# Attention into a soft mixture of experts: other bank shares for the value products, and sums moved off VectorE

## The chip, the cores and the metric

One core of a Trainium2 chip runs the program. Its engines work side by side, each through its own list of instructions in the order written: TensorE (PE in the rows; PEld is its weight load), VectorE (DVE), ScalarE (ACT), GpSimd (POOL); SyncE (SP) starts most transfers. Matrix products land in PSUM, which is cut into banks of 512 fp32 columns a partition; POOL works on SBUF only here. The metric is the device time of one execution in microseconds (us), lower is better.

## The reference

```python
def _attn_ref(q, kv, w_sr):
    kv_pool = kv.reshape(B, H // r, r, W // r, r, C).mean(axis=(2, 4))
    kv_flat = kv_pool.reshape(B, -1, C) @ w_sr      # 768 keys, used as values too
    s = (q @ k.transpose(0, 2, 1)) / sqrt(C)
    a = exp(s - s.max(-1)); a /= a.sum(-1) + 1e-09
    return a @ v

def _moe_ref(x, phi, w1, w2):
    logits = x @ phi                                 # 32 slots
    d = exp(logits - logits.max(0)); d /= d.sum(0) + 1e-09   # over all tokens
    slot_input = d.T @ x
    slot_out = relu(slot_input[e] @ w1[e]) @ w2[e]   # 8 experts, 4 slots each
    c = exp(logits - logits.max(1)); c /= c.sum(1) + 1e-09   # over the slots
    return c @ slot_out
```

There are 4 batches of 12288 queries with 128 channels (49152 tokens in all). The slot part needs the attention output of all tokens before any output can be written.

## The kernel before

Queries go in 96 blocks of 512 (index `i`), four blocks to a group of 16 tiles of 128 tokens (index `g`; 23 groups of four blocks, one of three, one of one: 25 in all, 0 to 24). For each block:

- `qk` (L553 to L562): scores, transposed, six key tiles of 128 keys by 512 queries, each from three fp32 products, into three PSUM tiles `s_0` to `s_2` of two banks each.
- `rowmax1` to `rowmax4` on DVE with one small product `rowmax_pe` (L598) between: the maximum of each query over all keys. `rowmax2` puts a small array into the last 80 columns of one of two shared banks `m0` and `m1`, `rowmax_pe` writes its 64 columns there (the key `pq` in the plan), `rowmax3` (L603) reads them back.
- `sub` (L616, DVE), `exp_hi` and `exp_t` (ACT), `plo` (L633, POOL): the exponentials as a sum of two fp16 arrays.
- `av_hi` and `av_lo` (L645 to L658): for each of the block's four tiles of 128 queries, 12 products with the high parts and 6 with the low part of the exponentials, 161 columns wide (row sum, 128 channels, 32 slot logits). They collect in `m0` or `m1`, two tiles (322 columns) to a bank (key `px`), and ACT copies each pair to `xl` with `av_evac` (L668).

For each group, `g0` to `g7a` keep running slot sums: the logits `LL`, their maximum over the group (`g2`, `g2c`, a small product `g3m` in a shared bank, key `pc`, then `g3` and `g3r` on DVE), rescaled exponentials (POOL, ACT), 32 products `g7m` (L834) in a shared bank (key `pd`) and the addition `g7a` to `acc` (DVE). For the output softmax, `k_max` (DVE), `k_sub` (POOL), `k_exp` (ACT), `k_sum` (L869, DVE), `k_add` (L874, ACT), `k_rec` (L879, DVE) and `k_mul` (L884, POOL) turn a group's logits into weights.

When all groups are through, the tail computes the slots' experts (`t_psi` to `t_slo`) and then 25 output chunks, one per group: transposes `c_t`, high and low parts `c_hi` (L1418, ACT) and `c_lo` (DVE), products `o_mm`, two copies `o_ev` (one half of each chunk by ACT, L1448, one by DVE, L1450), and a transfer of 1 MB (`o_dma`, L1468).

The order on PE, DVE, ACT and POOL is fixed when the program is built. The class `Plan` takes each piece of work with an estimated cost, a priority and its dependences, plays the engines against each other and writes the pieces down in the order in which they got their turn. `m0` and `m1` are handed out there too: `bank` chooses the one that is free first by the plan. A piece with `fill` waits for a gap until it is due. On the chip each engine then keeps that order whatever the pieces really take. `JOIN` says how many groups share one `k_add` and one `k_rec`.

Of the kernel before, what the change touches and what calls it, by code (L numbers as in the profile page):

```python
# [33 lines left out]
SPARE = 0.02  # L34


class Plan:
# [22 lines left out]
    def emit(self):  # L60
# [31 lines left out]
        def bank(key):  # L92
            found = []
            for b in range(len(banks)):
                if key[0] == "pq":
                    t = gone(banks[b])
                    beside = banks[b] is not None and banks[b][1][0] == "px" and t == inf
                    if beside:
                        t = summed.get(banks[b], inf)
                    found.append((max(t, gone(tops[b])), not beside, b))  # L100
                else:
                    found.append((max(gone(banks[b]), gone(tops[b])), False, b))
            return min(found)

        def acquire(n, now):
# [10 lines left out]
            if ops[n][0] == "ACT":  # L116
                for key in ops[n][11]:
                    if key[0] == "m" and key[1][0] == "px":
# [89 lines left out]
def attention_then_soft_moe(ctx: ExitStack, tc: tile.TileContext, qT, kv0, kvT, w_sr, w_srT, phi, w1, w2, outT):  # L208
# [111 lines left out]
    MRUN = {}  # L320
    NBK = BQ // Q32
# [16 lines left out]
    KEEP = 5  # L338
    SPAN = 2
    KPS = 2  # L340
    KSD = 2
# [3 lines left out]
    JOIN = (0, AHEAD, 12, EARLY)  # L345
# [10 lines left out]
    LATE = 6.0  # L356
# [278 lines left out]

    def av_tile(i, k):
        if k % 2 == 0 and i == NB - 1:
            PX[i, k // 2] = ps.tile([P, 2, BQ], F32, tag=f"s{k // 2}", name=f"px_{i}_{k}")[:, :, :VW]
        elif k % 2 == 0:
            px = mt([P, 512], f"px_{i}_{k}")  # L640
            PX[i, k // 2] = px[:, : 2 * VW].rearrange("p (n c) -> p n c", n=2)
        return PX[i, k // 2][:, k % 2, :]

    def av_hi(i, k, t0):
        _, vhi, vlo = VU[i // BPB]  # L645
        px = PX[i, k // 2][:, k % 2, :] if t0 else av_tile(i, k)
        ks = slice(k * P, (k + 1) * P)
        for t in range(t0, t0 + AVS):
            p = PP[i, t // TH][0][:, t % TH, ks]
            nc.tensor.matmul(px, p, vhi[:, t, :], start=(t == 0 and (i >= AHD or k % 2 == 0)), stop=False)  # L650
            nc.tensor.matmul(px[:, 1:], p, vlo[:, t, :], start=False, stop=False)  # L651

    def av_lo(i, k):
        vhi = VU[i // BPB][1]
        px = PX[i, k // 2][:, k % 2, :]
        ks = slice(k * P, (k + 1) * P)
        for t in range(NT):
            nc.tensor.matmul(px, PP[i, t // TH][1][:, t % TH, ks], vhi[:, t, :], start=False, stop=(t == NT - 1 and (i >= AHD or k % 2 == 1)))  # L658

    def av_evac(i, k):  # L660
# [3 lines left out]
        o = (i - GB[g][0]) * TB + 2 * k  # L664
        if i == NB - 2 and k == 0:
            nc.vector.tensor_copy(XL[g][:, o : o + 2, :], PX.pop((i, k)))
        else:
            nc.scalar.activation(XL[g][:, o : o + 2, :], PX[i, k], AF.Copy)  # L668
# [113 lines left out]
    def g3(g):  # L782
        d = G[g]
        c1 = sm2(g, "c1", [P, 1])
        nc.vector.tensor_reduce(out=c1, in_=d["pc"][:, :NQD], axis=X, op=ALU.max)
        d["gm"] = d["pc"][:, NS : 2 * NS]
        nc.vector.transpose(out=d["gm"], in_=c1.broadcast_to([P, NS]))

    def g3r(g):
        d = G[g]  # L790
        MRUN[g] = gp.tile([P, NS], F32, tag="mrun", name=f"mrun_{g}", bufs=3)
        if g == 0:
            nc.vector.tensor_copy(MRUN[g], d["gm"])
        else:
            nc.vector.tensor_tensor(out=MRUN[g], in0=MRUN[g - 1], in1=d["gm"], op=ALU.max)

# [41 lines left out]

    def g7a(g):
# [5 lines left out]
        nc.vector.tensor_tensor(out=acc, in0=acc, in1=G[g]["pd"][:, : C + 1], op=ALU.add)  # L845


    def k_max(g, u=None):
        o, n = GB[g][0] * TB, nt(g)
        if u is not None:  # L850
            o, n = o + u * TB, TB
# [12 lines left out]
    def k_sum(g, u=None):  # L864
# [4 lines left out]
        nc.vector.tensor_reduce(out=RM[:, o : o + n], in_=LL[:, o : o + n, :], axis=X, op=ALU.add)  # L869

# [167 lines left out]
    def group_ops(g):  # L1038
# [28 lines left out]
        def go(name, eng, cost, dep, f, acq=(), use=(), path=None, fill=False):  # L1067
            k[0] += 1
            due = base + step * k[0] + LATE if fill and not fast else None
# [26 lines left out]
        go("3c", "DVE", 0.42, [o["3m"]], g3, use=[mc], fill=True)  # L1096
        go("3", "DVE", 0.19, [o["3c"]] + ([ops["g3", g - 1]] if g else []), g3r, use=[mc], fill=True)
# [13 lines left out]
        go("7a", "DVE", 0.25, [o["7m"]] + prev, g7a, use=[md], fill=True)  # L1111
# [7 lines left out]
    def av_rest(i, k, m, p, prev):  # L1119
        los = [ops["lo", i, 0], ops["lo", i, 1]]  # L1120
        a2 = end_lo = op("PE", 6 * 0.072, 0.17, p + 0.8, prev + los, lambda: av_lo(i, k), use=[("plo", (i, 0)), ("plo", (i, 1)), m])
        if k % 2:
            g = GOF[i]
            first = i == GB[g][0] and k == 1
            x = ("xl", g)
            if i == NB - 1:
                v = k // 2
# [4 lines left out]
            ops["x", i, k // 2] = op(  # L1132
# [481 lines left out]
```

## Time and profile before

| what | value |
|---|---|
| median of 3 runs | 1062.12 us (1062.01 to 1062.18) |
| profiled execution, its own time | 1062.19 us |
| its span, first to last instruction | 1060.4 us |
| PE busy | 1027.6 us (97%) |
| DVE busy | 971.5 us (92%) |
| POOL busy | 872.5 us (82%) |
| ACT busy | 793.6 us (75%) |
| granted TensorE clock | 0.996 of full speed, the level of 2.4 GHz |

The span has three parts: a start of some 25 us, the 96 blocks until about 976 us, and the tail. The page's shares are means over all three. PE's busy time counts a product from its start to its end, and neighbours overlap, so a lost moment is read from the distance between two starts.

### The profile page before, as it was taken

The page shows a single profiled execution, that of the slowest core. Times are in us where ns is not written, and L with a number is a line of the kernel's source. Part 1 is how long each engine was busy: PE and PEld are TensorE (multiplying, and loading weights), DVE is VectorE, ACT ScalarE, POOL GpSimd, SP SyncE. Part 2 cuts the span into 40 slices and gives each one's busy share as a digit, 9 for nine tenths or more (in the row PEclk, how much of TensorE's full clock was granted, in tenths as well). Part 3 has the DMA queues.
Part 4 walks back from the last instruction along what each step waited for, and adds up shares of the span by engine and source line. Part 5 has one row for each costly group of instructions (what it writes and reads, how often), then busy time and mean ns, then how long its engine had stood idle before and what let it go on. Part 6 is the DMA issues. An engine that isn't in the chain of part 4 may idle for free.

```text
span 1060.4 us, 24836 instructions
## 1 busy us (share of the span) xinstructions
PE 1027.6 (97%) x10261; PEld 880.3 (83%) x10261; DVE 971.5 (92%) x1552; ACT 793.6 (75%) x1046; POOL 872.5 (82%) x509
## 2 busy tenths in 40 slices
PE   8999999999999999999999999999999999999994
PEld 5788888888888888888888888888888888888452
DVE  6989999999999999999999999999999999998774
ACT  3777887888777787788787787788787787776463
POOL 0789998889989988889989988889988999895800
PEclk9999999999999999999999999999999999999998
DMA  9234510120137320120146310120110110112598
GB/s 370 112 83 89 119 54 3 42 87 15 41 72 148 71 56 2 41 100 2 41 87 134 86 41 1 41 100 1 41 41 2 42 41 1 41 41 91 198 416 368
DMA packets 15729, 89.17 MB, mean 84 GB/s; under 512 B 1664, under 2 KB 1920, under 8 KB 9344
## 3 DMA queue, kind: packets, MB, share of 16 engines
q1 hardware_dynamic: 11728, 69.47, 17.8%
q0 software_dynamic: 3312, 17.70, 8.9%
q8 instruction: 81, 1.33, 0.5%
q10 hardware_dynamic: 576, 0.41, 0.1%
q14 instruction: 32, 0.26, 0.1%
HBM read 58.87 MB, written 25.17 MB: 79 GB/s over the span
## 4 chain that ended last, share of the span: by engine, by line
PE 86%; DVE 7%; DMA 3%; ACT 1%; issue 1%; POOL 0%; SPq 0%; DVEq 0%; ACTq 0%; POOLq 0%
PE m L650 15%; PE m L658 14%; PE m L651 14%; PE s L560 12%; PE s L562 12%; PE s L561 11%; DMA outT<-o 2%; PE m L834 2%; DVE r L578 2%; DVE t L616 2%; PE po L1434 1%; DMA kv<-kv 1%; PE m L1406 1%; DVE m L603 1%; PE m L465 1%
## 5 line engine op out<-in xcount | busy, mean ns | idle before, releaser
L633 POOL TENSOR_TENSOR plo<-t,phi 128x1536 f16<-128x1536 f32 x190 | 599.0, 3163 | 92.9 <-ACT t L628 84.0
L624 ACT ACTIVATE phi<-t 128x1536 f16<-128x1536 f32 x192 | 283.5, 1478 | 148.0 <-DVE t L616 148.0
L578 DVE TRANSPOSE_TENSOR_REDUCE r<-s 128x32 f32<-128x1024 f32 x289 | 354.0, 1234 | 8.4 <-PE s L562 1.6
L650 PE MATMUL m<-vhi,phi 128*128 128x161 f16 x2280 | 353.2, 234 | 8.2 <-DVE m L603 7.3
L651 PE MATMUL m<-vlo,phi 128*128 128x160 f16 x2280 | 352.4, 233 | 0.0
L616 DVE TENSOR_TENSOR t<-s,mb 128x1024 f32<-128x1024 f32 (+1 forms) x384 | 342.0, 950 | 6.2
L628 ACT ACTIVATE t<-t 128x1536 f32<-128x1536 f32 x192 | 283.1, 1476 | 1.2
L650 PEld LDWEIGHTS <-phi 128*128 128x128 f16 x2304 | 224.1, 98 | 21.7 <-issue 21.3
L560 PE MATMUL s<-qhi,khi 128*128 128x512 f32 x574 | 237.0, 413 | 0.6 <-DVE t L616 0.4
L651 PEld LDWEIGHTS <-phi 128*128 128x128 f16 x2304 | 225.1, 98 | 12.1 <-issue 10.6
L562 PE MATMUL s<-qhi,klo 128*128 128x512 f32 x574 | 224.6, 391 | 0.0
L561 PE MATMUL s<-qlo,khi 128*128 128x512 f32 x574 | 223.9, 390 | 0.0
L658 PE MATMUL m<-vhi,plo 128*128 128x161 f16 x2280 | 223.5, 234 | 0.0
L658 PEld LDWEIGHTS <-plo 128*128 128x128 f16 x2304 | 171.9, 98 | 2.8 <-issue 2.7
L550 POOL TENSOR_TENSOR qlo<-q,qhi 128x512 fp32r<-128x512 f32 x95 | 127.5, 1342 | 23.9 <-ACT qhi L545 23.9
L562 PEld LDWEIGHTS s<-qhi,klo 128*128 128x128 f32 x574 | 107.7, 188 | 23.7
L560 PEld LDWEIGHTS s<-qhi,khi 128*128 128x128 f32 x574 | 107.9, 188 | 21.7 <-issue 2.6
L561 PEld LDWEIGHTS s<-qlo,khi 128*128 128x128 f32 x574 | 108.2, 189 | 19.4 <-issue 0.7
L668 ACT ACTIVATE xl<-m 128x322 f32<-128x322 f32 x189 | 81.3, 430 | 50.4 <-PE m L658 44.1
L608 DVE STREAM_TRANSPOSE mb<-m 128x512 f32<-128x512 f32 x96 | 68.3, 712 | 3.3
L545 ACT ACTIVATE qhi<-q 128x512 fp32r<-128x512 f32 x96 | 59.5, 620 | 2.8 <-DMA q<-qT 2.7
L603 DVE TENSOR_REDUCE m<-m 128x16 f32<-128x64 f32 x96 | 21.5, 224 | 22.6 <-PE m L598 19.2
(196 smaller groups left out, 840.4 us busy)
## 6 DMA issues: line engine op xcount, KB each, us to landing
q<-qT SPq DMA_DIRECT2D x23, 1024.0 KB, 4.9
outT<-o SPq DMA_DIRECT2D x22, 1024.0 KB, 8.3
kva<-kvT POOLq DMA_DIRECT2D x9, 1536.0 KB, 11.6
kva<-kvT SPq DMA_DIRECT2D x3, 1536.0 KB, 12.8
kv<-kv SPq DMA_DIRECT2D x6, 512.0 KB, 6.2
w<-w SPq DMA_DIRECT2D x2, 1536.0 KB, 6.3
w<-w SPq DMA_DIRECT2D x4, 768.0 KB, 4.1
kva<-kva POOLq DMA_DIRECT2D x3, 768.0 KB, 10.8
```

The source lines that it names most:

```text
L550: eng.tensor_tensor(out=lo, in0=q_src(i), in1=hi.bitcast(F32), op=ALU.subtract)
L560: nc.tensor.matmul(s, khi[:, ks], hi, start=True, stop=False)
L561: nc.tensor.matmul(s, khi[:, ks], lo, start=False, stop=False)
L562: nc.tensor.matmul(s, klo[:, ks], hi, start=False, stop=True)
L578: nc.vector.tensor_reduce(out=MX[i][:, t : t + n, :].rearrange("p t b -> p (t b)"), in_=S[i, t // 2][:, u : u + n, :].rearrange("p t (b j) ...
L616: nc.vector.tensor_tensor(out=TT_[i, h][:, o : o + n, :], in0=S[i, t // 2][:, u : u + n, :], in1=MX[i].unsqueeze(1).broadcast_to([P, n, BQ ...
L624: nc.scalar.activation(hi, TT_[i, h], AF.Exp, scale=SCALE)
L628: nc.scalar.activation(t, t, AF.Exp, scale=SCALE)
L633: eng.tensor_tensor(out=lo, in0=TT_.pop((i, h)), in1=PP[i, h][0], op=ALU.subtract)
L650: nc.tensor.matmul(px, p, vhi[:, t, :], start=(t == 0 and (i >= AHD or k % 2 == 0)), stop=False)
L651: nc.tensor.matmul(px[:, 1:], p, vlo[:, t, :], start=False, stop=False)
L658: nc.tensor.matmul(px, PP[i, t // TH][1][:, t % TH, ks], vhi[:, t, :], start=False, stop=(t == NT - 1 and (i >= AHD or k % 2 == 1)))
```

## The change

1. The four tiles of a block share the banks as three and one (483 and 161 columns) instead of two and two (`part`, `px_of`, `av_evac`). The plan lets the row maxima's columns (`pq`) stand beside a single value tile, a `pc` or a `pd`, no longer beside a pair (`BESIDE`).
2. `k_sum` of groups 4 to 21 leaves DVE. A chain of five POOL additions per group, `k_tree`, takes its place; it may start once `g5m` of group 23 is done, that is, in the tail. `JOIN` goes from three shared steps to seven.
3. `g7a` of groups before 23 becomes a copy on ACT (`g7e`) and an addition on POOL.
4. The running slot maximum is kept as one column (`CM`): `g3r` takes a maximum of two columns and then the transpose into `MRUN`.
5. `k_max` of a group is two DVE instructions instead of four.
6. `g3m` of groups 1 to 20 waits for the third score tile five blocks on, and `g7m` for the last one six blocks on.

```diff
+BESIDE = ("pc", "pd")
...
-                    beside = banks[b] is not None and banks[b][1][0] == "px" and t == inf
+                    beside = banks[b] is not None and (banks[b][1][0] in BESIDE or banks[b][1][0] == "px" and banks[b][1][2] == 1) and t == inf
...
-    JOIN = (0, AHEAD, 12, EARLY)
+    JOIN = (0, AHEAD, 6, 9, 12, 15, 18, EARLY)
...
+    def part(i, k):
+        if i == NB - 1:
+            return k // 2, k % 2, 2
+        return (0, k, TB - 1) if k < TB - 1 else (1, 0, 1)
...
-            nc.scalar.activation(XL[g][:, o : o + 2, :], PX[i, k], AF.Copy)
+            nc.scalar.activation(XL[g][:, o : o + n, :], PX[i, k], AF.Copy)
...
     def g3r(g):
-        d = G[g]
+        if g:
+            nc.vector.tensor_scalar_max(CM[g], CM[g], CM.pop(g - 1))
         MRUN[g] = gp.tile([P, NS], F32, tag="mrun", name=f"mrun_{g}", bufs=3)
...
+        nc.vector.transpose(out=MRUN[g], in_=CM[g].broadcast_to([P, NS]))
...
+    def g7e(g):
+        d = G[g]
+        d["px"] = sm2(g, "pdx", [P, C + 1])
+        nc.scalar.activation(d["px"], d["pd"][:, : C + 1], AF.Copy)
...
-        nc.vector.tensor_tensor(out=acc, in0=acc, in1=G[g]["pd"][:, : C + 1], op=ALU.add)
+        nc.gpsimd.tensor_tensor(out=acc, in0=acc, in1=G[g]["px"], op=ALU.add)
...
+    def k_tree(g):
+        o, n = GB[g][0] * TB, nt(g)
+        t = gp.tile([P, TG, NS], F32, tag="D", name=f"ks_{g}")
+        a, w = LL[:, o : o + n, :], NS // 2
+        while w > 1:
+            b = t[:, :n, :w]
+            nc.gpsimd.tensor_tensor(out=b, in0=a[:, :, :w], in1=a[:, :, w : 2 * w], op=ALU.add)
+            a, w = b, w // 2
+        nc.gpsimd.tensor_tensor(
+            out=RM[:, o : o + n].unsqueeze(2), in0=a[:, :, :1], in1=a[:, :, 1:2], op=ALU.add
+        )
...
+    for g in range(1, FAST - 2):
+        e = GB[g][0] + GB[g][1] - 1
+        plan.ops[ops["g3m", g]][4].append(ops["qk", e + 5, AT3])
+        plan.ops[ops["g7m", g]][4].append(ops["qk", e + 6, NT - 1])
...
+    for g in trees:
+        ops["ks", g] = [op("POOL", 1.5, 0.1, T1 + 278 + 4 * g, [ops["ke", g], ops["g5m", FAST]], lambda g=g: k_tree(g), acq=[("D", ("ks", g))])]
```

What this does to the order of instructions, at three places. In the first two, PE around a row maximum: `rq` with a block's number is what `rowmax_pe` multiplies, `phi` and `plo` with a block's number are the exponentials' parts, and `m0` and `m1` are the two shared banks. Before, at the row maximum of block 46, after the second tile of block 44:

```order
L658 MATMUL m1_120<-vhi_1_3306,plo_44_1_6634 128x161
L598 LDWEIGHTS sel_h_109
L598 MATMUL m0_119<-rq_46_6764,sel_h_109 128x64 [waits DVE_49]
L650 LDWEIGHTS phi_44_0_6541
L650 MATMUL m0_119<-vhi_1_3306,phi_44_0_6541 128x161 [waits DVE_49]
L651 LDWEIGHTS phi_44_0_6541
L651 MATMUL m0_119<-vlo_1_3307,phi_44_0_6541 128x160
```

Now, at the same row maximum:

```order
L604 MATMUL m1_120<-rq_46_6751,sel_h_109 128x64 [waits DVE_49]
L674 LDWEIGHTS plo_44_0_6554
L674 MATMUL m0_119<-vhi_1_3362,plo_44_0_6554 128x161
...
L665 MATMUL m0_119<-vhi_1_3362,phi_44_0_6510 128x161
...
L674 MATMUL m0_119<-vhi_1_3362,plo_44_1_6605 128x161
L665 LDWEIGHTS phi_44_0_6510
L665 MATMUL m1_120<-vhi_1_3362,phi_44_0_6510 128x161 [waits DVE_49]
```

Before, the next product into the bank of the row maximum stood right behind it; now the second tile's low products and the whole third tile stand between, in the other bank.

The second place is PE at the slot maximum `cb` of group 5, which comes between tiles of block 26. Before, nothing of it stood there, and the bank of the row maximum was the next tile's:

```order
L598 MATMUL m0_119<-rq_28_4141,sel_h_109 128x64 [waits DVE_49]
L658 LDWEIGHTS plo_26_0_3961
L658 MATMUL m1_120<-vhi_1_3306,plo_26_0_3961 128x161
...
L658 MATMUL m1_120<-vhi_1_3306,plo_26_1_4033 128x161
L650 LDWEIGHTS phi_26_0_3933
L650 MATMUL m0_119<-vhi_1_3306,phi_26_0_3933 128x161 [waits DVE_49]
```

Now:

```order
L604 MATMUL m0_119<-rq_28_4127,sel_h_109 128x64 [waits Activation_49]
...
L794 MATMUL m0_119<-cb_5_4115,sel_bf_107 128x4 [waits Activation_49]
L794 LDWEIGHTS sel_bf_107
L794 MATMUL m0_119<-cb_5_4115,sel_bf_107 128x4 [waits Pool_49]
...
L674 MATMUL m1_120<-vhi_1_3362,plo_26_1_4034 128x161
L665 LDWEIGHTS phi_26_0_3932
L665 MATMUL m1_120<-vhi_1_3362,phi_26_0_3932 128x161 [waits Activation_49]
```

`m0` holds the row maximum and the slot maximum, so the single tile follows the three in `m1`, behind ACT's copy of the three.

The third place is the tail, on ACT and POOL. `RM` holds the sums of the output softmax (`128x32` is a `k_add` of two groups, `128x48` of three), `hs` are the experts' hidden values, `shi` the high part of the slots' outputs, `o` and `po` an output chunk with its number. ACT before:

```order
L862 ACTIVATE LL_115<-LL_115 128x512 [waits Pool_49]
L1325 ACTIVATE hs_14243<-ph_0_14190 128x512 [waits DVE_49,PE_49]
...
L1325 ACTIVATE hs_14243<-m0_119 128x512 [waits PE_49]
...
L1390 ACTIVATE shi_14339<-psq_14325,tsum_14284 128x128 [waits PE_49]
...
L1448 ACTIVATE o_2_14386<-po_2_1_14388 128x2x4x128 [waits DMAHW2_49,PE_49]
L1448 ACTIVATE o_1_14413<-po_1_1_14415 128x2x4x128 [waits DMASW1_49,DMASW7_49,DMASW0_49,PE_49]
```

ACT now:

```order
L1368 ACTIVATE hs_14211<-ph_0_14138 128x512 [waits DVE_49,PE_49]
L903 ACTIVATE RM_116<-RM_116,eps_95 128x32 [waits Pool_49]
L903 ACTIVATE RM_116<-RM_116,eps_95 128x16 [waits DVE_49]
L1368 ACTIVATE hs_14211<-m0_119 128x512 [waits PE_49]
...
L903 ACTIVATE RM_116<-RM_116,eps_95 128x48 [waits Pool_49]
L1433 ACTIVATE shi_14337<-psq_14316,tsum_14262 128x128 [waits PE_49]
...
L1491 ACTIVATE o_2_14388<-po_2_1_14390 128x2x4x128 [waits DMAHW2_49,PE_49]
L903 ACTIVATE RM_116<-RM_116,eps_95 128x48 [waits Pool_49]
L1491 ACTIVATE o_1_14420<-po_1_1_14422 128x2x4x128 [waits DMASW1_49,DMASW7_49,DMASW0_49,PE_49]
```

Six `k_add` that wait for POOL stand among the slots' chain and the output copies: one before the second `hs`, one before `shi`, one before the third chunk's copy, and, further down, one each before the copies of the seventh, the eleventh and the fifteenth chunk. POOL now, from the last slot work of group 23 on (`ks` with a group's number is a chain of additions):

```order
L828 TENSOR_TENSOR da_23_14112<-da_23_14112,sel1_101 128x32 [waits Activation_49]
L894 TENSOR_TENSOR ks_4_14196<-LL_115 128x16x16 [waits PE_49,Pool_49]
L894 TENSOR_TENSOR ks_4_14196<-ks_4_14196 128x16x8 [waits Pool_49]
...
L896 TENSOR_TENSOR RM_116<-ks_4_14196 128x16 [waits Pool_49]
L874 TENSOR_TENSOR LL_115<-LL_115,RM_116 128x512 [waits DVE_49]
...
L894 TENSOR_TENSOR ks_5_14227<-LL_115 128x16x16 [waits Pool_49]
...
L913 TENSOR_TENSOR LL_115<-LL_115,RM_116 128x512 [waits DVE_49]
```

Before, three `k_sub` and 21 `k_mul` stood here; now 18 chains of five additions stand among them, each addition waiting for the one before.

## Rows read from the trace of the kernel before

**Rows 1.** The page's part 1: busy time, share of the span, instructions.
```profile
PE 1027.6 (97%) x10261; PEld 880.3 (83%) x10261; DVE 971.5 (92%) x1552; ACT 793.6 (75%) x1046; POOL 872.5 (82%) x509
```

**Rows 2.** Busy time per stretch: PE, PEld, DVE, ACT, POOL, clock, DMA share, GB/s.
```profile
150.00:950.00 800.00, 792.66 (x8111) 701.56 (x8109) 759.80 (x1209) 628.60 (x823) 721.35 (x409) 1.00 0.18 49
1000.00:1050.00 50.00, 43.98 (x382) 24.17 (x380) 37.24 (x41) 31.60 (x41) 4.95 (x6) 1.00 1.01 417
```

**Rows 3.** Waits of PE, whole span: total us, times, longest.
```profile
PE m L650 <- DVE m L603: 7.3, 23, 0.3
```

**Rows 4.** Timeline around a row maximum: start, us, engine, line, operation [idle before].
```profile
961.14 0.19 PE L598 MATMUL m<-rq,sel_h 128*128 128x64 f16 x1
...
961.37 0.23 DVE L603 TENSOR_REDUCE m<-m 128x16 f32<-128x64 f32 x1
...
961.65 0.23 PE L650 MATMUL m<-vhi,phi 128*128 128x161 f16 x1 [0.32 <-DVE m L603]
```

**Rows 5.** Timeline, another row maximum, then a tile without one.
```profile
508.22 0.59 PE L658 MATMUL m<-vhi,plo 128*128 128x161 f16 x6
...
508.70 0.23 PE L650 MATMUL m<-vhi,phi 128*128 128x161 f16 x1
...
508.85 0.44 ACT L668 ACTIVATE xl<-m 128x322 f32<-128x322 f32 x1 [1.20 <-PE m L658]
...
509.54 0.60 PE L658 MATMUL m<-vhi,plo 128*128 128x161 f16 x6
...
509.98 0.23 PE L650 MATMUL m<-vhi,phi 128*128 128x161 f16 x1
```

**Rows 6.** Groups of ACT by shape: count, busy us, mean ns, idle before.
```profile
L628 ACT ACTIVATE t<-t 128x1536 f32<-128x1536 f32 x192 | 283.1, 1476 | 1.2
...
L668 ACT ACTIVATE xl<-m 128x322 f32<-128x322 f32 x189 | 81.3, 430 | 50.4 <-PE m L658 44.1 <-PE m L598 5.5
...
L1448 ACT ACTIVATE o<-po 128x1024 f32<-128x1024 f32 x22 | 22.5, 1024 | 18.1 <-DMA outT<-o 9.7 <-PE po L1434 7.6 <-ACT chi L1418 0.8
...
L1418 ACT ACTIVATE chi<-m 128x512 fp32r<-128x512 f32 x19 | 11.3, 597 | 1.0
```

**Rows 7.** Groups of DVE by shape: the output softmax's sums.
```profile
L869 DVE TENSOR_REDUCE RM<-LL 128x8 f32<-128x256 f32 x44 | 17.9, 408 | 0.0
```

**Rows 8.** Single lines of POOL: duration ns min/median/max, first and last start, forms.
```profile
L800 POOL TENSOR_TENSOR D<-LL,mrun x24: 1003/1278/1732, 105.9 to 976.4; 128x512 f32<-128x512 f32 x23, 128x384 f32<-128x384 f32 x1
```
```profile
L805 POOL TENSOR_TENSOR da<-mrun,mrun x23: 242/259/495, 144.8 to 977.3; 128x32 f32<-128x32 f32 x23
```
```profile
L857 POOL TENSOR_TENSOR LL<-LL,RM x25: 400/1049/1455, 124.0 to 985.3; 128x512 f32<-128x512 f32 x23, 128x384 f32<-128x384 f32 x1, 128x128 f32<-128x128 f32 x1
```

**Rows 9.** Timeline of DVE in the tail: two instructions, the second of which needs the first.
```profile
974.57 0.17 DVE L757 TENSOR_REDUCE cmt<-cm 128x1 f32<-128x12 f32 x1
974.77 0.23 DVE L685 TENSOR_SCALAR cq<-quad,cmt 128x4 f32<-128x4 f32 x1
```

**Rows 10.** Timeline of PE in the tail: slot products of group 23.
```profile
979.97 0.87 PE L834 MATMUL m<-xl,D 128*32 128x129 f32 x24
```

**Rows 11.** Timeline of POOL in the tail.
```profile
982.48 1.05 POOL L857 TENSOR_TENSOR LL<-LL,RM 128x512 f32<-128x512 f32 x1 [3.01 <-DVE sm L1299]
...
984.49 1.19 POOL L857 TENSOR_TENSOR LL<-LL,RM 128x384 f32<-128x384 f32 x2
985.64 19.31 POOL L884 TENSOR_TENSOR LL<-LL,RM 128x512 f32<-128x512 f32 x20
```

**Rows 12.** Timeline of ACT in the tail.
```profile
986.23 0.31 ACT L874 ACTIVATE RM<-RM,eps 128x16 f32<-128x16 f32 x1 [0.15 <-DVE RM L869]
987.19 0.60 ACT L1325 ACTIVATE hs<-m 128x512 f32<-128x512 f32 x1 [0.65 <-PE m L1322]
...
993.28 0.37 ACT L1390 ACTIVATE shi<-psq,tsum 128x128 fp32r<-128x128 f32 x1 [1.16 <-PE psq L1384]
```

**Rows 13.** Timeline of SP in the tail: the first output transfers.
```profile
995.96 0.94 SPq L1462 DMA_DIRECT2D outT<-o  x2
```

## What the change will do: the prediction

> **What bounds the kernel now.** I read the page's shares first, then stretches, then PE's waits, then timelines. PE is busy 97% of the span [rows 1], and between 150 and 950 us 99% (792.7 of 800), DVE 95% there, POOL 90%, ACT 79% [rows 2]. So the blocks run at PE's pace as long as DVE keeps up. PE's waits show how little is left: the one that recurs is PE at a value tile, held by DVE's `rowmax3`, 23 times, 7.3 us in all [rows 3]. A timeline shows it: `rowmax_pe` writes into a bank, the next value tile wants that bank at once, and PE starts it only when DVE has read the maxima out, 0.51 us later [rows 4]. From about 996 us on the stretch is another one: DMA is full (share 1.01, 417 GB/s), PE, DVE and ACT have gaps, and POOL hardly works, 5 of 50 us [rows 2]. There the end is set by when the first output leaves [rows 13] and whether the transfers, 1.049 MB each and so 2.51 us at 417 GB/s, ever run dry.
>
> **The banks (edit 1).** Where the next tile follows `rowmax_pe` directly, the distance of starts is 0.51 us [rows 4]; the small product's 64 columns need 0.03 of it, at the pace of 161 columns in 0.07 (six in 0.44) [rows 5]. So 0.48 is lost, 23 times: 11.0 us. In 64 more places six low products stand between; there they and the next start are 0.48 us apart instead of 0.44 for a tile without a maximum [rows 5]: 0.04 each, 2.6 us. In the new order 0.7 us of products or more stand between in 93 of 96 blocks, and `rowmax3` is done 0.46 us after `rowmax_pe` starts [rows 4]; both losses go, 13.6 us.
>
> The new order has losses of its own. Two early blocks still have the tile right behind the maximum: 2 x 0.48 = 1.0 us. In eight groups (0, 4 to 9, 22) the other bank holds a row and a slot maximum, so the single tile goes into the bank that the three tiles have just left, and PE waits for ACT to copy it. The last low product takes 0.23 us, ACT starts 0.04 after its end (508.81 to 508.85) [rows 5], a copy of 483 columns lies on the line from 322 columns (0.43) to 512 (0.60) at 0.57 [rows 6], and PE starts 0.05 after the reader's end (961.60 to 961.65) [rows 4]. That is 0.89 us from start to start where 0.07 is usual: 0.82 lost, eight times 6.6 us, and 0.4 in one early place with six products between. The ends: nothing, if ACT is through before, and 0.82 + 1.48 if ACT has just begun an exponential [rows 6]; I take 0.82, since ACT idles a fifth of this stretch [rows 2]. Sum on PE: 13.6 - 1.0 - 7.0 = 5.6 us less.
>
> **DVE's relief (edits 2 to 5).** DVE loses 36 sums of 0.41 us [rows 7], 14.7 us, and the smaller pieces of the other edits. I count it at nothing: what PE waits for from DVE is in the 7.3 us already [rows 3]. POOL's addition to `acc` (128x129, between 0.26 and 0.47 by the lines below) and ACT's copy add half a us per group each, on engines with 10% and 21% idle. Edit 6 moves 32 products between places; the same breaks between kinds of products remain, so nothing, between -1 and +1 us.
>
> **The chains on POOL (edit 2).** This decides. 18 chains of five additions, each needing the one before, run where POOL was free. Sizes are 256, 128, 64, 32 and 16 elements a partition. The nearest rows are POOL instructions with two full inputs: 512 elements in 1.278 us, 32 in 0.259 [rows 8], so 2.12 ns an element, and 0.735 + 0.463 + 0.327 + 0.259 + 0.225 = 2.0 us. An instruction that needs the one before starts 0.03 us after its end (on DVE, 974.74 to 974.77) [rows 9]: five times, 2.15 us a chain. The ends: 1.75 by the line with a broadcast input (0.400 at 128, 1.049 at 512) without gaps, and 2.8 if the three smallest take as long as the longest small one, 0.495 [rows 8]. I take 2.15; two full inputs is what they have.
>
> They may start when group 23's slot products are through, 980.9 [rows 10]. In POOL's list stand among them three `k_sub` (2.2 us) and, up to chain 21, `k_mul` for 14 full groups at 1.0 us, and 2.2 for groups 22 to 24 [rows 11]. ACT works its list in order, and a `k_add` that waits for POOL holds what stands behind it. Three places count:
> - Before `shi`: chain 8 ends at 980.9 + 5 x 2.15 + 2.2 + 2.0 = 995.9, `k_add` takes 0.3, so `shi` starts at 996.2 instead of 993.28 [rows 12]: 2.9 us late, and all output with it.
> - Before the third chunk's copy: chain 11 ends at 980.9 + 8 x 2.15 + 2.2 + 5.0 = 1005.3; with `k_add` 0.3 and the copy 1.0 [rows 6, 12] the transfer can go at 1006.6. At full DMA it went at 995.96 + 2 x 2.51 = 1001.0 [rows 13]: 5.6 us late.
> - Before the fifteenth: chain 21 ends at 980.9 + 38.7 + 2.2 + 16.2 = 1038.0; `k_add`, one `c_hi` (0.6) and the copy make 1040.0, against 995.96 + 14 x 2.51 = 1031.1: 8.9 us late.
> Late transfers can't be made up at full DMA, so the largest counts: 8.9 us, that is 18 times the chain less 29.8. At 1.75 us a chain the third chunk decides, some 2.5 us; at 2.8 it is 20.
>
> On this edit the pages speak too. By rows the sum of a group costs DVE two instructions of 0.41 us and POOL five in 2.15. The Trainium skill (GPSIMD Engine Reference, section 4.1, Engine selection) has a reduction along the free dimension on VectorE. Left on DVE as the rule has it, the sum would be 1062.2 - 5.6 = 1056.6; moved, it is the one below. The trace bears the rule out as far as the prices go, and against it stands only that DVE is nearly full in the blocks.
>
> **Sum.** 1062.19 us of the profiled execution (1.8 around the span; 0.07 over the median) - 5.6 + 8.9 = 1065.5 us.
>
> **Rivals.**
> - Faster: the chains fit. The point is where 18 times the chain less 29.8 equals PE's gain less 2.1, at 1.85 us a chain. For it: broadcast inputs run that fast, and the plan counted 1.5. Against it: the additions have two real inputs. With 1.75 us and half the waits for the copies (3.3 us less) it is 1062.2 - 8.9 + 2.5 = 1055.8.
> - No change: a chain of 1.95 us or so, late by 5.3, takes back PE's gain: 1062.
> - Heavier chains: narrow, strided pieces cost more, no row shows any below 32 elements; at 2.5 us, 15.2 late: 1071.8.
> - The banks don't deliver: the wait only changes its cause, from DVE's read to ACT's copy, if each copy stands behind an exponential. Eight times 1.48 more is 11.8: 1077. Against it: ACT idles before these copies, 44.1 us in all for PE [rows 6]. Small.
> - DVE was the true bound and its relief shows: 15 us less work and more would shorten blocks beyond PE's stalls. PE's 99% in the stretch speaks against it.
>
> **How the numbers follow.** What a measurement can tell from no change is 0.2%, 2.1 us. My forecast and its near neighbours (1064.3 to 1069) 0.38, heavier chains or failing banks (above 1069) 0.15: slower 0.53. No change 0.20. Faster 0.27, most of it between 1053 and 1060. The likeliest case's own range is 1061 to 1070. The range of 8 in 10 goes from the fast rival to the heavier chains: 1054 to 1073.
>
> **What would show it.** PE's wait for `rowmax3` at value tiles falls from 23 times to two or three; a wait of PE for ACT's copy to `xl` appears some eight times at 0.67 us idle. The blocks end 5 to 6 us earlier. In the tail, POOL is full until about 1045 less that shift; ACT's waits for POOL stand at L903, summing to more than 5 us; the DMA share falls below 1 after the second and the fourteenth chunk. Wrong would be: a chain under 1.85 us, no wait at L903, or blocks that end over 10 us earlier.

## The result, and the profile after

The changed kernel takes 1073.01 us (median of 4 runs, 1072.48 to 1073.75), the kernel before 1062.07 (4 runs, 1061.99 to 1062.18): a ratio of 1.0103, 95% interval 1.0086 to 1.0121. It is 10.9 us slower, where 3.3 were forecast. The profiled execution took 1072.48 us and its span is 1070.7, 10.3 more than before. Line numbers below are the changed kernel's unless a run is named: `rowmax_pe` L604, `rowmax3` L609, `rowmax4` L614, `sub` L622, score products L566 to L568, value products L665, L666 (high) and L674 (low), copies to `xl` L684, chains L894 and L896, `k_add` L903, the reciprocal behind it L908, output copies L1491 (ACT) and L1493 (DVE).

The page's busy shares first, which answer to [rows 1]:

```profile
PE 1031.9 (96%) x10261; PEld 880.8 (82%) x10261; DVE 952.8 (89%) x1452; ACT 806.7 (75%) x1073; POOL 915.9 (86%) x622
```

DVE has 18.7 us less, POOL 43.4 more, PE the same number of products. By stretches, with the columns of [rows 2]:

```profile
150.00:950.00 800.00, 794.03 (x8134) 701.24 (x8133) 741.92 (x1114) 641.39 (x847) 732.83 (x433) 1.00 0.18 50
...
1000.00:1050.00 50.00, 41.65 (x320) 21.89 (x317) 31.53 (x36) 26.75 (x37) 39.09 (x77) 0.89 0.85 350
```

In the blocks PE is busy 1.4 us more of 800, so little was won; in the tail the DMA share is 0.85 instead of 1.01: there 15% of the DMA's time went unused. The two can be split at one instruction: the last slot product, group 24's, right behind those of group 23, starts at 980.9 us before and at 979.6 after, 1.4 earlier. The tail behind it is 11.7 us longer.

**The blocks.** PE's waits (total us, times, longest) no longer have `rowmax3` among their larger rows. What stands there, for the whole span:

```profile
PE m L665 <- ACT xl L684: 5.4, 9, 0.7
```

That is the single tile in the bank that three tiles have just left: PE waits until ACT has copied the three. A timeline (start, us, engine, line, operation, idle before) of one such place:

```profile
300.03 0.52 PE L674 MATMUL m<-vhi,plo 128*128 128x161 f16 x5
...
300.59 0.57 ACT L684 ACTIVATE xl<-m 128x483 f32<-128x483 f32 x1 [1.17 <-PE m L674]
301.22 0.23 PE L665 MATMUL m<-vhi,phi 128*128 128x161 f16 x1 [0.66 <-ACT xl L684]
```

From the last low product's start (300.32, five in 0.07 steps from 300.03) to the next tile are 0.90 us, and 0.82 of it is lost. But a wait that the page hardly shows has come as well. Another timeline, around the row maximum of block 59:

```profile
606.22 0.22 DVE L596 SCALAR_TENSOR_TENSOR rq<-m,quad_h 128x64 f16<-128x64 f32 x1
...
606.84 0.19 PE L604 MATMUL m<-rq,sel_h 128*128 128x64 f16 x1
...
607.08 0.22 DVE L609 TENSOR_REDUCE m<-m 128x16 f32<-128x64 f32 x1 [0.30 <-PE m L604]
607.34 0.71 DVE L614 STREAM_TRANSPOSE mb<-m 128x512 f32<-128x512 f32 x1
...
608.08 2.42 DVE L622 TENSOR_TENSOR t<-s,mb 128x1024 f32<-128x1024 f32 x3
...
608.71 0.60 PE L674 MATMUL m<-vhi,plo 128*128 128x161 f16 x6
...
609.45 0.47 PE L566 MATMUL s<-qhi,khi 128*128 128x512 f32 x1
```

The first score product of the next block writes the bank that the first subtraction reads. From `rowmax_pe` to that score product are 2.61 us: `rowmax3`, the transposition, a subtraction of two tiles, and the hand-overs. PE has 2.23 us of products between, so it stands for 0.35. The trace draws a value product 0.23 us long although the next starts after 0.07, so most of such a wait is hidden in it: it is read from start to start (609.07, where the last low product starts, to 609.45, usually 0.03).

Counted so over all PE rows from the first `rowmax_pe` to the last slot product, each kind of break (a change from one kind of product to another) beyond its usual distance, in us:

| lost on PE | before | after |
|---|---|---|
| tile right behind `rowmax_pe` | 11.3 | 1.0 |
| tile behind low products or a slot maximum (a copy) | 4.0 | 6.8 |
| score product behind value or slot products | 1.9 | 5.6 |
| `rowmax_pe` itself, for `rq` | 1.8 | 3.4 |
| sum | 18.9 | 16.8 |

The rows differ by 2.1 us, and PE got there 1.4 us sooner; the 0.7 between them lie outside these four rows and were not followed.

**The tail.** POOL's timeline, the first chain with what follows, the starts of the next two, and the end of the last:

```profile
979.81 0.73 POOL L894 TENSOR_TENSOR ks<-LL 128x256 f32<-128x256 f32 x1 [1.61 <-PE m L845]
980.62 1.17 POOL L894 TENSOR_TENSOR ks<-ks 128x128 f32<-128x128 f32 x3
981.86 0.22 POOL L896 TENSOR_TENSOR RM<-ks 128x16 f32<-128x16 f32 x1
982.04 2.20 POOL L874 TENSOR_TENSOR LL<-LL,RM 128x512 f32<-128x512 f32 x3
...
984.19 0.73 POOL L894 TENSOR_TENSOR ks<-LL 128x256 f32<-128x256 f32 x1
...
986.54 0.73 POOL L894 TENSOR_TENSOR ks<-LL 128x256 f32<-128x256 f32 x1
...
1038.73 0.21 POOL L896 TENSOR_TENSOR RM<-ks 128x16 f32<-128x16 f32 x1
1039.99 4.06 POOL L913 TENSOR_TENSOR LL<-LL,RM 128x512 f32<-128x512 f32 x4 [1.05 <-DVE RM L908]
```

From a chain's start to that of the `k_sub` behind it are 2.23 us (979.81 to 982.04). Its five additions by shape (count, busy us, mean ns, idle before):

```profile
L894 POOL TENSOR_TENSOR ks<-LL 128x256 f32<-128x256 f32 x18 | 13.2, 732 | 1.9 <-PE m L845 1.6
L894 POOL TENSOR_TENSOR ks<-ks 128x128 f32<-128x128 f32 x18 | 8.2, 455 | 1.4
L894 POOL TENSOR_TENSOR ks<-ks 128x64 f32<-128x64 f32 x18 | 5.8, 321 | 1.4
L894 POOL TENSOR_TENSOR ks<-ks 128x32 f32<-128x32 f32 x18 | 4.3, 239 | 1.4
L896 POOL TENSOR_TENSOR RM<-ks 128x16 f32<-128x16 f32 x18 | 3.9, 215 | 1.4
```

ACT's waits for POOL there, and ACT's timeline around chain 21:

```profile
ACT RM L903 <- POOL RM L896: 15.7, 6, 3.7
```

```profile
1034.44 1.02 ACT L1491 ACTIVATE o<-po 128x1024 f32<-128x1024 f32 x1 [0.44 <-PE po L1477]
1038.98 0.35 ACT L903 ACTIVATE RM<-RM,eps 128x64 f32<-128x64 f32 x1 [3.52 <-POOL RM L896]
1039.23 0.58 ACT L1461 ACTIVATE chi<-m 128x512 fp32r<-128x512 f32 x1
1039.71 1.01 ACT L1491 ACTIVATE o<-po 128x1024 f32<-128x1024 f32 x1
```

ACT stands still for 3.52 us with a finished chunk behind `k_add`, and DVE stands with it, since the reciprocal needs `k_add`:

```profile
1039.36 0.55 DVE L908 RECIPROCAL RM<-RM 128x64 f32<-128x64 f32 x1 [3.51 <-ACT RM L903]
1039.84 0.69 DVE L1465 TENSOR_TENSOR clo<-m,chi 128x512 fp32r<-128x512 f32 x1
1040.45 1.22 DVE L1493 COPY o<-po 128x1024 f32<-128x1024 f32 x1
```

The transfer of that chunk leaves at 1041.7. The windows beside it show the price (clock, DMA share and GB/s are the last three columns):

```profile
1037.50:1040.00 2.50, 0.17 (x2) 0.00 (x0) 0.64 (x2) 1.02 (x3) 1.22 (x5) 1.00 1.00 419
1040.00:1042.50 2.50, 1.72 (x14) 0.77 (x15) 2.50 (x4) 1.66 (x3) 2.50 (x3) 0.78 0.17 72
1042.50:1045.00 2.50, 2.50 (x16) 1.64 (x16) 1.05 (x2) 1.18 (x2) 1.55 (x2) 0.54 1.02 419
```

The first output, which answers to [rows 13], leaves 2.3 us later than before. ACT's `shi` starts as much later (995.59, where [rows 12] have 993.28), behind a `k_add` that waited 3.31 us for POOL:

```profile
998.26 0.94 SPq L1505 DMA_DIRECT2D outT<-o  x2
```

So of 10.3 us in the span 2.3 are the later first output, and 8.0 are time in which the transfers ran dry behind it.

### The profile page after: what moved, and what is told of

It reads as the page before. It is cut to its first block, busy times and chain, and to the rows that moved or that the text cites. A ratio compares the mean times of both kernels' runs of the same rounds, so it can differ in the third digit from the quotient of the medians.

```text
span 1070.7 us, 24913 instructions
## 1 busy us (share of the span) xinstructions
PE 1031.9 (96%) x10261; PEld 880.8 (82%) x10261; DVE 952.8 (89%) x1452; ACT 806.7 (75%) x1073; POOL 915.9 (86%) x622
## 5 line engine op out<-in xcount | busy, mean ns | idle before, releaser
L665 PE MATMUL m<-vhi,phi 128*128 128x161 f16 x2280 | 354.6, 234 | 6.1 <-ACT xl L684 5.4
L666 PE MATMUL m<-vlo,phi 128*128 128x160 f16 x2280 | 353.6, 233 | 0.0
L622 DVE TENSOR_TENSOR t<-s,mb 128x1024 f32<-128x1024 f32 (+1 forms) x384 | 342.2, 949 | 7.1
L665 PEld LDWEIGHTS <-phi 128*128 128x128 f16 x2304 | 224.0, 98 | 26.6 <-issue 23.9
L566 PE MATMUL s<-qhi,khi 128*128 128x512 f32 x574 | 236.7, 412 | 2.2 <-DVE t L622 0.9
L666 PEld LDWEIGHTS <-phi 128*128 128x128 f16 x2304 | 225.3, 98 | 7.4 <-issue 7.3
L568 PE MATMUL s<-qhi,klo 128*128 128x512 f32 x574 | 224.7, 392 | 0.0
L674 PE MATMUL m<-vhi,plo 128*128 128x161 f16 x2280 | 223.3, 234 | 0.0
L684 ACT ACTIVATE xl<-m 128x483 f32<-128x483 f32 (+1 forms) x189 | 82.5, 437 | 156.2 <-PE m L674 146.8
L674 PEld LDWEIGHTS <-plo 128*128 128x128 f16 x2304 | 172.2, 98 | 1.0 <-issue 0.8
L566 PEld LDWEIGHTS s<-qhi,khi 128*128 128x128 f32 x574 | 107.9, 188 | 26.6 <-PE m L674 4.1
L568 PEld LDWEIGHTS s<-qhi,klo 128*128 128x128 f32 x574 | 107.7, 188 | 23.9
L614 DVE STREAM_TRANSPOSE mb<-m 128x512 f32<-128x512 f32 x96 | 68.3, 711 | 3.3
L594 DVE TENSOR_REDUCE m<-r 128x16 f32<-128x96 f32 x96 | 31.7, 330 | 15.2 <-PE m L845 8.4
## 6 DMA issues: line engine op xcount, KB each, us to landing
kva<-kvT POOLq DMA_DIRECT2D x9, 1536.0 KB, 10.9
```

Of the source, the lines that this page charges most:

```text
L566: nc.tensor.matmul(s, khi[:, ks], hi, start=True, stop=False)
L568: nc.tensor.matmul(s, klo[:, ks], hi, start=False, stop=True)
L622: nc.vector.tensor_tensor(out=TT_[i, h][:, o : o + n, :], in0=S[i, t // 2][:, u : u + n, :], in1=MX[i].unsqueeze(1).broadcast_to([P, n, BQ ...
```

## The experiments

Each run's median stands beside that of the kernel before on the same chip (1062.2 to 1062.5 us).

**Which part costs what.** The changed kernel with its sums back on DVE:

```diff
-    JOIN = (0, AHEAD, 6, 9, 12, 15, 18, EARLY)
+    JOIN = (0, AHEAD, 12, EARLY)
...
-        if AHEAD <= g < EARLY:
-            trees.append(g)
-        elif g < EARLY:
+        if g < EARLY:
```

> The changed kernel with the sums over slots put back on VectorE (two instructions of 0.41 us a group) and k_add joined as before: every other edit stands. Theory A (the two parts add: PE's gain in the blocks is only 1.4 us, and the chains cost the tail 11 to 12 us): 1060.5 to 1062.5 us against 1062.1 before, PE's start of group 23's last slot product at 979 to 981, output from 995 on with the DMA share at 1.0. Rival B (the blocks gained only because VectorE was relieved; with 14.7 us put back it holds PE more often): 1064 us or more, with PE's waits for VectorE's subtraction at the score products in every group instead of 12 times 0.3 us. Rival C (what the chains' extra work on the list of GpSimd did to the blocks is what ate the gain): 1057 to 1059 us.

Measured: 1061.58 us, ratio 0.9992 (0.9984 to 1.0001); DMA share 1.01 from 1000 to 1050 us. The reverse, `k_tree` and the new `JOIN` put into the kernel before:

> The kernel before with the sums alone moved to chains on GpSimd in the tail, and k_add joined as in the changed kernel. Theory A: the blocks run as before (last rowmax at 961 +- 1 us), the tail loses what the changed kernel's tail loses: 1072 to 1075 us. Rival B (VectorE's relief is worth several us in the blocks): last rowmax at 957 or earlier, 1066 to 1070 us. Rival D (the chains cost little by themselves, it is the mix with the other edits): under 1066 us.

Measured: 1074.03 us, 1.0108 (1.0094 to 1.0122), last `rowmax_pe` at 960.8. Theory A held in both: the chains by themselves cost 11.4 to 11.6 us, all of it in the tail, and DVE's relief by 14.7 us moved the last `rowmax_pe` by 0.3 us in the kernel before. In the changed kernel it moved by 2.0, of which 1.1 lie at the start, before the blocks (the profiled execution of the first run is 1.0 us over its median). And the bank edit alone, in the kernel before:

```diff
+BESIDE = ("pc", "pd")
...
+        return (0, k, TB - 1) if k < TB - 1 else (1, 0, 1)
...
-        return PX[i, k // 2][:, k % 2, :]
+        return PX[i, v][:, j, :]
```

> The kernel before with the bank edit alone (three tiles and one, the banks' rules), all sums and maxima where they were. By the order PE has the tile right behind rowmax_pe 2 times instead of 23, and 4 same-bank places at 0.82 us. Theory S: 13.8 us of waits for rowmax3 go, 3.3 + 1.0 come, and little else: 1052 to 1056 us. Rival L (VectorE's chain from rq over rowmax3 and rowmax4 to the subtractions sets the score products; rowmax_pe stands later, so PE waits at the scores): 1059 to 1063 us.

Measured: 1069.34 us, 1.0058 (1.0046 to 1.0071): slower than both theories had it. PE's loss behind `rowmax_pe` fell from 11.3 to 1.0 us, and that at score products rose from 1.9 to 13.4, in 40 places (12.6 of it behind low products). So the waits of [rows 3] moved and grew, by some 2 us over the four kinds of the table. That is less than half of the loss: of the 5.5 us that the span is longer, 2.9 lie behind the last `rowmax_pe`, where PE waits 1.7 us for POOL's `D` before slot products and 1.5 us for ACT's copy to `xl` before a slot maximum. These two waits were not followed further. The other edits on DVE and the set places give back 7 to 8 us (this run less the first: 7.8 by the medians, 7.0 by the ratios).

**What holds the score products.** First more room on DVE: the run before, and its `rowmax1` reads one tile of each pair, so that half of the keys is left out of the maximum.

```diff
+        n = 1 if i else n
...
-        nc.vector.tensor_reduce(out=r1, in_=MX[i].rearrange("p t b -> p b t"), axis=X, op=ALU.max)
+        nc.vector.tensor_reduce(out=r1, in_=(MX[i][:, ::2, :] if i else MX[i]).rearrange("p t b -> p b t"), axis=X, op=ALU.max)
```

> The kernel before with the bank edit alone (1069.3 us), every list as there, but VectorE's first maxima read one of the two score tiles of a pair (half of the keys is left out of the row maximum): 3 instructions of 1.21 us a block become 0.65, so VectorE has 1.7 us of 9.9 more room in each block. Theory L (the waits that left rowmax3 stand at the score products, behind VectorE's subtractions, only because VectorE is that full): the 12.6 us at score products go, 1054 to 1058 us. Rival Q (PE's waits there come from the order on PE itself or from another engine): 1066 us or more.

> The kernel before with the same half maxima, every list as before. Theory L: PE's waits for rowmax3 behind rowmax_pe depend on the place and stay (10.3 us), score products didn't wait before, so the room on VectorE is worth little: 1060 to 1062.5 us. Rival V (VectorE's work by itself is the bound of the blocks, whatever the banks): 1050 us or less.

Measured: 1065.72 us (1.0032, 1.0020 to 1.0043) with the banks, 1060.47 (0.9982, 0.9973 to 0.9990) in the kernel before. My theory L fell: the first was to be at 1054 to 1058 us, and the rival's 1066 is near. DVE idled (rows of 150 to 950 us, banks with whole maxima, then with half):

```profile
150.00:950.00 800.00, 792.39 (x8102) 698.92 (x8102) 751.02 (x1206) 636.21 (x821) 716.05 (x405) 1.00 0.18 49
```

```profile
150.00:950.00 800.00, 792.60 (x8106) 700.20 (x8104) 627.73 (x1207) 636.67 (x823) 717.52 (x405) 1.00 0.18 49
```

and PE's loss at score products stayed at 13.4 us in the same 40 places. DVE now waited 72.9 us for PE at `rowmax3`:

```profile
DVE m L607 <- PE m L602: 72.9, 78, 1.5
```

All that the room brought is the wait for `rq` (2.7 to 0.6 us; the profiled spans differ by 2.0). What is left is theory K: a chain of fixed length that begins where PE's list has `rowmax_pe`. It is tested by lengthening it where DVE has room, in the kernel before with half maxima:

```diff
         nc.vector.transpose(out=m, in_=MX[i].unsqueeze(2).broadcast_to([P, NBK, Q32]))
+        if i:
+            nc.vector.transpose(out=m, in_=MX[i].unsqueeze(2).broadcast_to([P, NBK, Q32]))
```

> The kernel before with half maxima (1060.5 us, VectorE idle a fifth of the blocks) and rowmax4's transposition done twice in each block, 0.74 us more between rowmax_pe and the first subtraction; the lists are the same otherwise. Theory K (the chain rowmax_pe, rowmax3, rowmax4, first subtraction has a fixed length, 2.6 us in the traces, and PE waits at the first score product behind it for what its own products between, 2.95 or 2.56 us, don't cover): 3.35 less 2.95 in some 70 blocks and 3.35 less 2.56 in some 25, 45 to 50 us in all, 1103 to 1111 us. Theory L (only VectorE's sum of work counts; it has 125 us of room and gets 70 more): 1060 to 1064 us.

Measured: 1097.75 us (1.0335, 1.0319 to 1.0351), 37.3 over the same kernel with one transposition. A timeline of one block:

```profile
610.07 0.19 PE L599 MATMUL m<-rq,sel_h 128*128 128x64 f16 x1
...
610.30 0.22 DVE L604 TENSOR_REDUCE m<-m 128x16 f32<-128x64 f32 x1 [0.94 <-PE m L599]
610.56 0.71 DVE L609 STREAM_TRANSPOSE mb<-m 128x512 f32<-128x512 f32 x1
611.31 0.71 DVE L611 STREAM_TRANSPOSE mb<-m 128x512 f32<-128x512 f32 x1
612.05 3.55 DVE L619 TENSOR_TENSOR t<-s,mb 128x1024 f32<-128x1024 f32 x4
613.42 0.47 PE L560 MATMUL s<-qhi,khi 128*128 128x512 f32 x1
```

613.42 less 610.07 is 3.35 us: 2.61 and 0.74. PE's loss at score products went from 1.9 to 38.1 us, in 92 blocks, 0.34 to 0.42 in most of them. From `rowmax_pe` to the score product are 3.35 to 3.43 us in 91 of 95 blocks now; in the kernel before 74 of them had 3.00 to 3.02. Theory K holds. The expected 45 to 50 were too many for the places that I had at 2.56 us of cover: they lost as little as the others. They are those with the tile right behind `rowmax_pe`, and the kernel before shows why:

```profile
566.52 0.20 PE L598 MATMUL m<-rq,sel_h 128*128 128x64 f16 x1
567.04 0.23 PE L650 MATMUL m<-vhi,phi 128*128 128x161 f16 x1 [0.32 <-DVE m L603]
...
569.54 0.47 PE L560 MATMUL s<-qhi,khi 128*128 128x512 f32 x1
```

The 0.5 us that PE waits for `rowmax3` are part of the same 3.0 us. While PE waits there, the chain to the score product runs on, so the wait is cover too.

**Taking the copies' waits away.** With `JOIN` single and the right price (below), three numbers of the plan, each altered alone, change how often the single tile follows in its own bank:

```diff
-AVD = 2.0
+AVD = 2.2
```

> The kernel with single joins and the plan's price of 2.28 (1062.2 us), with one more number of the plan altered (AVD 2.2 for 2.0, the lag at which value products rank behind their block), by which the single tile goes right behind the three tiles in their own bank 1 time instead of 8. Theory S (each such place costs 0.82 us of PE, and nothing takes it back): 1055.5 to 1058 us. Rival L (PE and VectorE pass the row maxima round in a loop; what PE no longer waits for a copy it waits at rowmax_pe or at a score product): 1060.5 to 1063 us, same-bank waits gone, PE's waits at score products grown.

```diff
-    SL = 0.5
+    SL = 0.3
```

> The same base with another number of the plan altered (SL 0.3 for 0.5, the slack given to a group's steps), by which the same-bank places fall from 8 to 2. Theory S: 6 x 0.82 = 4.9 us less, 1056 to 1058.5 us. Rival L: 1060.5 to 1063 us.

```diff
-        r2 = op("DVE", 0.58, 0.06, T0 + 2, [ops["r", i]], lambda i=i: rowmax2(i), acq=[("m", ("pq", i)), ("rq", i)], use=[("r6", i)], hot=True, raw=0.1, gap=GAP)
+        r2 = op("DVE", 0.58, -0.3, T0 + 2, [ops["r", i]], lambda i=i: rowmax2(i), acq=[("m", ("pq", i)), ("rq", i)], use=[("r6", i)], hot=True, raw=0.1, gap=GAP)
```

> The base of single joins, and the plan takes rq to be ready 0.36 us sooner (latency -0.3 for 0.06), so PE's list has rowmax_pe about one slice of value products earlier; same-bank places 4 instead of 8. Theory P (the late place of rowmax_pe is what makes PE wait 12 x 0.36 us at score products): those waits go and half the same-bank waits: 1054 to 1057 us. Rival L (in most blocks rowmax_pe already starts 0.06 us behind rq; placed earlier PE waits there): 1062 us or more, PE's waits for rq 0.1 to 0.3 us in some 60 blocks.

> The changed kernel with all sums on VectorE (1061.6 us) and SL 0.3: same-bank places 9 fall to 2. Theory S: 7 x 0.82 = 5.7 us less, 1056 us. Theory L (the waits turn up at score products): 1061 to 1063 us.

| run | behind `rowmax_pe` | copies | scores | `rq` | median us | ratio, 95% |
|---|---|---|---|---|---|---|
| base (single joins) | 1.0 | 6.8 | 5.7 | 3.3 | 1062.19 | 0.9997 (0.9988 to 1.0006) |
| AVD 2.2 | 1.0 | 1.2 | 16.1 | 6.0 | 1079.75 | 1.0165 (1.0151 to 1.0179) |
| SL 0.3 | 1.9 | 2.0 | 8.9 | 3.5 | 1062.07 | 0.9998 (0.9990 to 1.0007) |
| `rq` 0.36 sooner | 1.0 | 3.2 | 6.7 | 26.0 | 1086.75 | 1.0227 (1.0213 to 1.0241) |
| SL 0.3, sums on DVE | 1.9 | 2.2 | 8.8 | 3.3 | 1060.76 | 0.9986 (0.9977 to 0.9994) |

Theory S missed in its three runs and theory P in the one with `rq` sooner; rival L's ranges took in two of the four and missed AVD 2.2 by 17 us. With SL 0.3 the copies cost 4.8 us less and the scores 3.2 more. `rowmax_pe` set sooner in PE's list waits for `rq` instead, in 90 blocks. With AVD 2.2 the losses named explain 7.5 of 17.6 us; another 6 lie between the first and second score product, and the rest is open, since that number moves many lists.

**The tail: price and joins.** The plan counted 1.5 us for a chain:

```diff
-        ops["ks", g] = [op("POOL", 1.5, 0.1, T1 + 278 + 4 * g, [ops["ke", g], ops["g5m", FAST]], lambda g=g: k_tree(g), acq=[("D", ("ks", g))])]
+        ops["ks", g] = [op("POOL", 2.28, 0.1, T1 + 278 + 4 * g, [ops["ke", g], ops["g5m", FAST]], lambda g=g: k_tree(g), acq=[("D", ("ks", g))])]
```

> The changed kernel with one number altered: the plan counts 2.28 us for a chain (as the trace shows) instead of 1.5, so ScalarE's list has its k_add behind more copies to o. Same chains, same work on every engine. Theory A1 (the chains themselves have room; what costs is that ScalarE's and VectorE's lists were written for chains of 1.5 us, so copies of finished output stand behind sums that are late): 1063 to 1067 us, first output 1 to 3 us earlier than 998.3, the waits of ScalarE for GpSimd at k_add 15.7 us now, under 6 us then. Rival A2 (GpSimd's work, 18 chains and 24 products of 1.05 us in a row, is too long for the output whatever the lists say): 1071 to 1074 us.

Measured: 1067.51 us, 1.0045 (1.0033 to 1.0058), half a us over theory A1's range. First output at 995.2, ACT's waits at `k_add` 1.7 us instead of 15.7. The DMA share is still 0.88 between 1000 and 1050. From the first output to the end are 70.5 us, where the kernel before has 64.4. Of these 6 us 2.6 are seen as a wait in POOL's own list, where `k_mul` needs a joined group's reciprocal:

```profile
POOL LL L913 <- DVE RM L908: 2.6, 2, 1.6
```

So the price was 5.5 of the 10.9 us. With the price, one group to a join:

```diff
-    JOIN = (0, AHEAD, 6, 9, 12, 15, 18, EARLY)
+    JOIN = (0, AHEAD) + tuple(range(5, EARLY)) + (EARLY,)
```

> As the run before, and k_add and the reciprocal for one group at a time instead of two to four, so no chunk waits for the sums of groups that it doesn't need. GpSimd can hand out group g at 979.8 + 2.2 + 3.33 x (g - 3) us, the output needs it at about 998 + 2.51 x g less the 5 us that the chunk spends on PE, ScalarE and VectorE: with 18 chains at 3.33 us the first is later from about group 23 on, so hardly ever. Theory A1: 1061 to 1064 us, DMA dry for under 2 us after the first output. Rival A2: 1069 us or more.

Measured: 1062.19 us, 0.9997 (0.9988 to 1.0006). The joins were the other half, 5.3 us. These are the same 18 chains, and the transfers don't run dry:

```profile
1000.00:1050.00 50.00, 43.73 (x369) 23.92 (x367) 38.08 (x52) 34.14 (x52) 39.22 (x77) 1.00 1.01 418
```

So POOL's work as such has room; what cost 11 us is where the lists, ACT's above all, wait for it. With chains only for groups 9 to 21 (groups 4 to 8 summed on DVE), and SL 0.3:

> The kernel with the price of 2.28, single joins and SL 0.3 (1062.1 us), with chains only for groups 9 to 21; groups 4 to 8 are summed on VectorE in the blocks. So no chain stands ahead of shi on ScalarE's list. Theory T (with the DMA full, the time is the first output's plus 64.5 us, and chains ahead of shi cost the first output about 1 us): first output at 995 us, 1060 to 1061.5 us. Rival: the five groups' sums on VectorE lengthen the blocks by as much, 1062 us.

Measured: 1061.83 us, 0.9998 (0.9989 to 1.0007). The first output left at 995.7, with all chains at 995.8, with none (SL 0.3, sums on DVE) at 994.7, each behind a last slot product at 979.5 or 979.6. So chains do cost it about 1 us, as theory T has it, but leaving out five of them gave nothing back. The edit did not do what I expected of it: the chains of groups 9 to 11 moved up, and their `k_add` stand ahead of `shi` instead. The last of them holds it in ACT's timeline:

```profile
992.87 0.31 ACT L903 ACTIVATE RM<-RM,eps 128x16 f32<-128x16 f32 x1 [1.53 <-POOL RM L896]
993.08 0.35 ACT L1433 ACTIVATE shi<-psq,tsum 128x128 fp32r<-128x128 f32 x1
```

With no chains `shi` starts at 992.00, behind its product. So T's condition, no chain ahead of `shi`, was not met and its time stays untried; that the span ends 64.3 to 64.5 us behind the first output holds in this run, in the one without chains and in the kernel before.

**The fewest waits of known price.** Sums on DVE as in the first run, and

```diff
-    SL = 0.5
+    SL = 0.2
...
-                "DVE", dve(n * BQ), 0.08, T0 - 4 + 0.63 * t, [r4] + ([ops["s", i, t0]] if t else []), lambda i=i, t=t, n=n: sub(i, t, n),
+                "DVE", dve(n * BQ), 0.3, T0 - 4 + 0.63 * t, [r4] + ([ops["s", i, t0]] if t else []), lambda i=i, t=t, n=n: sub(i, t, n),
```

> The changed kernel with all sums on VectorE and two numbers of the plan altered (SL 0.2; a subtraction is taken to end 0.22 us later), chosen so that, by the order, waits of known price are fewest: same-bank places cost 0.9 us (7.1 with the plan as it was), tiles right behind rowmax_pe none (1.0), score products with under 2.6 us of cover 7.2 us (6.6). Theory K: 21.4 - 14.9 = 6.5 us less than 1061.6, of which the run with SL 0.3 had 0.8 where 3.2 were worked out; 1056 to 1060 us. Rival: the waits turn up at rowmax_pe for rq or elsewhere, 1061 to 1063 us.

Measured: 1060.15 us, 0.9980 (0.9971 to 0.9989). Behind `rowmax_pe` PE lost 0.0, at copies 3.3, at scores 6.4, for `rq` 4.8: 14.6 in all, 3.1 less than in the first run, and the last slot product starts at 978.8. Fewer waits of known price did pay, by 1.4 of the 6.5 us worked out; it is 0.2% faster than the kernel before and just missed theory K's range. Breaks ahead of slot maxima and slot products, which had no price, cost some 2.2 us more than in the first run.

## Why the prediction missed

The span was to be 3.3 us longer and is 10.3. Term by term:

- **Behind `rowmax_pe`: right.** 13.6 us were to go and 1.0 to stay; 10.3 net went there, and 3.6 of the small losses behind low products.
- **Same-bank places: right.** 8 at 0.82 us, 6.6, were forecast; there are 5 at 0.82 behind low products and 3 at 0.77 behind a slot maximum, 6.4.
- **"Sum on PE: 13.6 - 1.0 - 7.0 = 5.6 us less": the step that failed.** A wait was credited with nothing late behind it. `rowmax_pe` now has its cover (products that PE can run meanwhile) on the side of `rowmax3`, and lacks it on the side of the score product: 3.7 us more there and 1.6 more at `rowmax_pe` itself. The gain is 1.4 us, 4.2 short. The trace of the kernel before had it: [rows 4] begin the chain, and a score product 3.0 us behind `rowmax_pe`, in the places of [rows 3] with 0.5 of wait among them, leaves only 0.4 to give.
- **"I count it at nothing" (DVE's relief): right for the sums, wrong for the rest.** The banks alone make the kernel 6 to 7 us slower; with the other edits and without the chains it is at 0.9992 of before, no change that can be told. Which of the other edits gives that back was not tried.
- **Chains: the instructions right, the gaps not.** Sizes of 256 to 16 take 0.732, 0.455, 0.321, 0.239 and 0.215 us, 1.96 where 2.0 was worked out from [rows 8]. Between dependent ones POOL leaves 0.08 us, not DVE's 0.03 of [rows 9]: 2.23 us to the next start where work that doesn't need the chain follows, and 2.35 where the next chain does (984.19 to 986.54), not 2.15. From the first chain's start to chain 21's end are 59.1 us; 57.1 were forecast.
- **"`k_add`, one `c_hi` and the copy": one engine too few.** The copy's other half is DVE's, and DVE's list waits at the reciprocal: from the end of chain 21 to the transfer are 2.8 us, not 2.0.

4.2 + 2.0 + 0.8 = 7.0, the difference of the spans. In the tail what was to show did show: ACT's waits at `k_add`, the DMA share below 1 at the third chunk (it was to leave at 1006.6 and left at 1006.4) and at the fifteenth. That the third came out to 0.2 us is luck in part: the chains started 1.1 us sooner than forecast and took 0.9 longer up to there. The blocks were to end 5 to 6 us earlier; the last slot product came 1.4 earlier. None of the three signs of being wrong came; all three stood for a faster kernel. The rule cited from the Trainium skill (GPSIMD Engine Reference, section 4.1, Engine selection), by which such a reduction belongs on VectorE, agrees with the first two runs: on DVE it costs the blocks at most 2 us, on POOL the tail 11.4. But the run with single joins shows that the place in the lists, more than the engine, made the price; what stays in DVE's favour is 0.6 us there, within the noise, and 1.3 with SL 0.3. Of the rivals, "DVE was the true bound" is out: 127 us less of its work between 150 and 950 us made the kernel before 1.9 us faster. "The banks don't deliver" came true by another mechanism than the one named: no copy stood behind an exponential, the score products waited. "Heavier chains" had nearly the right time for the wrong reason, since the narrow additions were cheap.

## What to carry to other kernels

A wait on one engine is one end of a loop: before its time is booked as won, follow the data on to where the same engine next needs it, and subtract the work between the two from the chain's fixed length (here 2.6 us). The wait itself counts as such work: take it away, and what it covered comes to light. Work moved to an idle engine costs what waits for it in other engines' lists: look at what stands behind the first instruction that reads its result, on every engine that must wait, and give the planner the measured price.

## What the runs showed of the hardware

- A dependent instruction follows 0.08 us behind the end of the one before on POOL (1.4 us of idle in 18 gaps, in each of four rows), and 0.03 on DVE ([rows 9]). One that doesn't need it starts 0.04 before that end (982.04, behind an addition from 981.86 for 0.22).
- Small two-input additions on POOL go on falling in price below 32 elements a partition: 0.239 us at 32, 0.215 at 16.
- In the changed kernel's tail TensorE's granted clock fell behind gaps in its work. It had been busy 1.1 and 1.5 of 2.5 us, then ran at half speed, the level of 1.2 GHz:

```profile
992.50:995.00 2.50, 1.10 (x10) 0.87 (x9) 0.10 (x1) 0.00 (x0) 2.27 (x5) 1.00 0.00 0
995.00:997.50 2.50, 1.51 (x13) 0.72 (x13) 1.78 (x5) 1.57 (x5) 2.03 (x7) 0.91 0.00 0
997.50:1000.00 2.50, 2.36 (x18) 1.50 (x16) 2.15 (x6) 1.64 (x3) 2.50 (x4) 0.50 0.39 151
1000.00:1002.50 2.50, 2.50 (x12) 0.82 (x12) 1.22 (x1) 1.02 (x1) 2.19 (x6) 0.50 0.69 272
```

Not every gap did it: busy 1.0 of 2.5 us from 1005.0 on, TensorE had the full clock in the next 2.5. With single joins the mean from 1000 to 1050 us is 1.00 again. What part of the 8 us of dry transfers the clock made was not tried.
